# Value-weight chunks, gate scales, the phi maximum and the next attention's steps at other places in a fused attention and mixer kernel

## The chip, the cores and the metric

The kernel runs on one core of one Trainium2 chip. The metric is the device time of one execution in microseconds (us). Three runs of the kernel before gave 1181.19, 1183.59 and 1186.07 us, so the median is 1183.59 us.

## The reference, cut to what matters

There are eight batch entries of 576 rows. Each goes through three blocks, one after the other. The comments on shapes are for B = H = 8, S = 576 and D = 64.

```python
# attention through 32 memory slots per head
a = softmax(phi, axis=memory)                      # 8 8 576 32
k_m, v_m = a^T k, a^T v                            # 8 8 32 64
x = softmax(q k_m^T / 8) v_m                       # 8 8 576 64, then 8 576 512

# token mixer and a feed-forward block
u = x + (x^T U V)^T                                # U 576 32, V 32 576
x = u + relu(u w_ch1) w_ch2                        # 512 to 2048 to 512

# spatial gate
h = relu(x w_in)                                   # 512 to 1024
u, v = h[:, :512], h[:, 512:]
v_s = w_spatial layernorm(v) + b_spatial           # over the 576 rows
out = (u * v_s) w_out
```

## The kernel before, in words

All products run in float16 pairs: each operand is split into a high and a low half, and three matmuls (the list `HI`) make one product. So an eviction from PSUM is mostly two instructions, a scaled copy to the high half on ScalarE (ACT) and a scalar-tensor-tensor for the low half on VectorE (DVE).

The batch entries follow each other on TensorE (PE), in a loop over `b`. From b = 2 on all have the same stages:

- `st_phase` (L893 to L1004), twice, for the first and second half (`th`) of the 576 rows. It makes the hidden layer (the products at L933, evicted at L937 to L945 and L920/L921) and the seven products of a Strassen scheme (L899). Between these, fillers call `step(nxt)`, which issues the next piece of the next entry's attention, a generator `att` (L552 to L705). In the first half every second call of `pfill` makes a step, and in the second half `late` makes one on every second call once `y_finish` has ended.
- The value and gate halves of w_in in the order of `V_ORDER`: `v_tile` (L1083, L1086, with statistics on DVE), `v_norm` (L1139 to L1146), `u_half` (L1157, L1161), and in between the last steps of the attention.
- `spatial` (L1180 to L1207), eight pieces d of 1.7 us of matmuls each (four for each half of the rows; L1194 to L1197). A piece is finished by DVE L1202 and L1203, ACT L1204 and DVE L1205, one after the other. `g_scale` makes the gate's scale of a half: a small matmul at L159 that spreads a maximum, DVE L161, GpSimd (POOL), DVE L174 and POOL again.
- `out_half` (L1209 to L1222), four output pieces for each half.

In the last two stages stand the four value-weight chunks of the next entry: `z_chunk` (L722 to L747), 24 small matmuls at L735 into two PSUM tiles of the tag `at`, which has three buffers, evicted by two ACT instructions (L746) and two DVE instructions (L747). Each chunk then lets SP load the next piece of weights. Chunks 0, 1 and 2 are issued after pieces 0, 1 and 5 of `spatial`, chunk 3 after two of the first output pieces.

`pre(b + 2)` makes the generator of the entry after the next and runs it to its first `yield`: the maximum of phi over the rows (DVE L556, 1152 columns) and two products with the identity into a `t1k` tile (L559). The next step begins with the matmul L563, which reads this `t1k`, and DVE L565, which subtracts.

The program is recorded in this order, but a scheduler orders the instructions of each engine outside `manual_schedule` blocks. So the phi maximum, whose input is there early, was moved ahead, into the norms of the values. `tc.issue_after` holds an instruction behind another on its engine.

Of the kernel before, what the change touches and what calls it, by code (L numbers as in the profile page):

```python
# [13 lines left out]
ALU = mybir.AluOpType  # L14
AX = mybir.AxisListType
# [15 lines left out]
def mixer_kernel(  # L31
# [219 lines left out]
    AT = {}  # L251
# [300 lines left out]
    def att(b):  # L552
        a = AT[b]
        sc = a["sc"] = tp.tile([128, 24], F32, tag="sc", name="sc", bufs=2)
        mx = sc[:, 0:2]
        dve.tensor_reduce(out=mx, in_=a["phiT"], axis=AX.X, op=ALU.max)  # L556
        dgx = t1k()
        for g in range(2):
            dve.tensor_scalar(out=dgx[:, g * 128:(g + 1) * 128], in0=ident, scalar1=sc[:, g:g + 1],  # L559
                              scalar2=None, op0=ALU.mult)  # L560
        yield
        mxb = at_tile()
        pe.matmul(mxb[:, 0:256], ones32, dgx, start=True, stop=True)  # L563
# [605 lines left out]
    def g_scale(b, th):  # L1169
# [7 lines left out]
        ps2(pool, sgt, sgt, 2.0 ** 13, ALU.mult)  # L1177
        ps2(pool, isg, mg, 2.0 ** -13, ALU.mult, C("rso"), ALU.mult)

    def spatial(b, th, fill):  # L1180
        a = AT[b]
        vn = a["vn"]
        sl = slice(th * TH, (th + 1) * TH)
        if th == 0:
            a["ghl"] = tp.tile([128, 4, 2, S], F16, tag="Y", name="ghl")
        ghl = a["ghl"]
        sgt = a["ysc"][:, th * 8 + 6:th * 8 + 7]
        for d in range(4):
            ds = slice(d * 128, (d + 1) * 128)
            ps = mm_tile()[:, 0:TH]  # L1190
            i = 0
            for s in range(4):
                for x, y in HI:
                    pe.matmul(ps, vn[:, s, x, ds], wsh[:, s, th, 1 - y, :], start=(i == 0), stop=False)  # L1194
                    i += 1
            pe.matmul(ps, vn[:, 4, 0, ds], wsh[:, 4, th, 1, :], start=False, stop=False)
            pe.matmul(ps, vn[:, 4, 0, ds], wsh[:, 4, th, 0, :], start=False, stop=True)  # L1197
            if th == 0 and d in (0, 2):
                g_scale(b, d // 2)
            t = tmp()[:, 0:TH]  # L1200
            u2 = a["u2"][:, d, sl]
            dve.scalar_tensor_tensor(out=t, in0=ps, scalar=C("cvs"), in1=bb[:, sl], op0=ALU.mult, op1=ALU.add)  # L1202
            dve.tensor_tensor(out=u2, in0=t, in1=u2, op=ALU.mult)  # L1203
            act.activation(ghl[:, d, 0, sl], u2, func=ACTF.Identity, scale=sgt)  # L1204
            dve.scalar_tensor_tensor(out=ghl[:, d, 1, sl], in0=u2, scalar=sgt, in1=ghl[:, d, 0, sl],  # L1205
                                     op0=ALU.mult, op1=ALU.subtract)
            fill()  # L1207

    def out_half(b, th, ds=range(4)):  # L1209
# [225 lines left out]

    def pre(b):
        if b < B:
            gen[b] = att(b)
            next(gen[b])

# [94 lines left out]
    for b in range(B):  # L1535
        nxt = gen.get(b + 1, iter(()))
        if b == 0:
            y1, a1 = batch0()
        elif b == 1:
            sq = s_prep()  # L1540
            w1_phase(b, 0, nofill)

            def both():
                step(nxt)
                next(sq, None)

            y0 = w2_phase(b, 0, lambda: step(nxt), lambda f: fl.until(s2, min(f + 3, 16)))
            w1_phase(b, 1, nofill, y_finish(b, 0, *y0))
            y1 = w2_phase(b, 1, both)
            drain(sq)  # L1550
            load_s4()
            load_ws()
        else:
            nf = [0]

            def every(n, g):
                def f():
                    nf[0] += 1
                    if nf[0] % n == 0:
                        g()  # L1560
                return f

            y0 = st_phase(b, 0, lambda: step(nxt), every(2, lambda: step(nxt)))
            yf = y_finish(b, 0, *y0)

            def late():
                if next(yf, "end") == "end":
                    nf[0] += 1
                    if nf[0] % 2 == 0:
                        step(nxt)  # L1570

            y1 = st_phase(b, 1, nofill, late)
            drain(yf)
# [3 lines left out]
        for op in V_ORDER.split():  # L1577
            if op == "y":
                for _ in y_finish(b, 1, *y1):
                    pass  # L1580
            elif op[0] == "v":
                s = int(op[1])
                vt[s] = v_tile(b, s)
                vf()
            elif op[0] == "n":
                v_norm(b, int(op[1]), *vt[int(op[1])])
            else:
                u_half(b, int(op[1]), (int(op[2]),), vf)
        if b == 0:
            fl.finish(so)  # L1590
            vfill = lambda dt: fl(dt, a1, s1, s2)
            vf = lambda: vfill(0.1)
        else:
            drain(nxt)
            if b + 2 < B:
                load_att(b + 2)
            nz = [0]

            def vf():
                nz[0] += 1  # L1600
                if nz[0] in (1, 2, 6) and b + 1 < B:
                    z_chunk(b + 1, min(nz[0] - 1, 2), at_tile)
        spatial(b, 0, vf)
        spatial(b, 1, vf)
        if b == 0:
# [3 lines left out]
            fl.finish(so)  # L1609
            fl.finish(s1)  # L1610
        pre(b + 2)
        out_half(b, 0, range(0, 2))
        if b and b + 1 < B:
            z_chunk(b + 1, 3, at_tile)
        out_half(b, 0, range(2, 4))
        if b + 2 < B:
            step(gen[b + 2])
        for op in Z_ORDER.split():
            if op[0] == "o":
                out_half(b, 1, (int(op[1]),))  # L1620
            elif b == 0:
                z_chunk(1, int(op[1]))
        if b == 0:
            store()
        elif b + 2 < B:
            load_w1(0)
# [63 lines left out]
```

## Time and profile before

| what | us |
|---|---|
| median of three runs | 1183.59 |
| the profiled execution's own time | 1181.76 |
| its span, first to last instruction | 1180.0 |
| PE busy with matmuls | 1131.9 (96%) |
| DVE busy | 846.4 (72%) |
| ACT busy | 611.0 (52%) |
| POOL busy | 85.3 (7%) |

The profile is of one execution; times in it are microseconds from the span's start. A row of the timeline gives an instruction's start, its duration, the engine, the line, the operation and in brackets how long the engine stood idle just before and what ended that. Neighbouring instructions of one kind are merged, with their count. PEclk is the granted TensorE clock, 1.00 for 2.4 GHz and 0.50 for 1.2 GHz, as a mean over the stretch. Entry 3 (b = 3) runs from about 502 to 641 us; its norms, gate and output stages lie between 580 and 641 us.

### The profile page before, as it was taken

The numbers are of one execution on the slowest core, as the hardware profiler recorded it, in microseconds if no ns is written. First come the engines' busy times: TensorE is split into PE (matmuls) and PEld (weight loads), VectorE is DVE, ScalarE is ACT, GpSimd is POOL, SyncE is SP. The second block draws the span as 40 slices with busy tenths as digits, with TensorE's granted clock in tenths as the row PEclk, the third lists the DMA queues.
The fourth block names the chain that finished last, engine by engine and source line by source line (L and its number), as shares of the span: only waits on it lengthen the run. The fifth ranks groups of instructions, "written<-read, shape, count | busy, mean of one in ns | idle before, by whom it ended". The sixth has DMA issues, their size and how long they took to land.

```text
span 1180.0 us, 28899 instructions
## 1 busy us (share of the span) xinstructions
PE 1131.9 (96%) x12015; PEld 886.3 (75%) x12015; DVE 846.4 (72%) x2217; ACT 611.0 (52%) x1308; POOL 85.3 (7%) x316
## 2 busy tenths in 40 slices
PE   8899989999999999999989999999999999899998
PEld 6467757677668986688857987679866888579867
DVE  6767787878776777678675787757867677656854
ACT  4768754736546345454354453553544633644543
POOL 3001010000010001000010000100010000100000
PEclk9999999999999999999999999999999999999999
DMA  9879740241435230441325313252313303030211
GB/s 349 317 261 354 240 186 11 103 142 56 159 108 176 71 132 21 173 132 49 132 87 186 88 32 135 91 189 75 115 38 140 126 24 124 31 118 2 79 45 41
DMA packets 54852, 145.69 MB, mean 123 GB/s; under 512 B 7808, under 2 KB 37248, under 8 KB 43584
## 3 DMA queue, kind: packets, MB, share of 16 engines
q1 hardware_dynamic: 54208, 143.16, 34.7%
q8 instruction: 94, 1.54, 0.5%
q10 hardware_dynamic: 512, 0.67, 0.2%
q14 instruction: 38, 0.31, 0.1%
HBM read 120.32 MB, written 23.49 MB: 122 GB/s over the span
## 4 chain that ended last, share of the span: by engine, by line
PE 65%; DVE 19%; ACT 8%; DMA 3%; POOL 2%; issue 2%; ACTq 0%; POOLq 0%; DVEq 0%
PE mm L899 20%; PE mm L933 9%; PE mm L1217 7%; PE mm L1194 6%; PE mm L1086 4%; PE mm L794 3%; PE at L629 2%; PE mm L854 2%; PE at L578 2%; DVE tiny L1092 2%; PE mm L771 1%; PE mm L817 1%; PE at L735 1%; ACT gw L1139 1%; DVE yhl L1053 1%
## 5 line engine op out<-in xcount | busy, mean ns | idle before, releaser
L899 PE MATMUL mm<-gw,w2r 128*128 128x144 f16 x2304 | 169.0, 226 | 1.8 <-DVE gw L945 1.8
L899 PEld LDWEIGHTS <-w2r 128*128 128x128 f16 x2304 | 152.4, 98 | 7.4 <-issue 2.4
L933 PE MATMUL mm<-apr,z 128*128 128x288 f16 x1152 | 155.4, 286 | 2.6 <-ACT wsr L937 2.6
L933 PEld LDWEIGHTS <-z 128*128 128x128 f16 x1152 | 109.8, 98 | 31.8 <-issue 6.2
L899 PE MATMUL mm<-gw,wa 128*128 128x144 f16 x1728 | 128.8, 226 | 0.0
L937 ACT ACTIVATE wsr<-mm 128x288 f32<-128x288 f32 x192 | 78.1, 407 | 80.1 <-DVE gw L921 44.1
L899 PEld LDWEIGHTS <-wa 128*128 128x128 f16 x1728 | 111.6, 98 | 3.6 <-issue 1.0
L1194 PE MATMUL mm<-wsr,gw 128*128 128x288 f16 x768 | 110.2, 294 | 1.7 <-DVE gw L1140 1.1
L1194 PEld LDWEIGHTS <-gw 128*128 128x128 f16 x768 | 74.5, 100 | 32.3 <-issue 8.1
L1217 PE MATMUL mm<-ghl,wa 128*128 128x288 f16 x768 | 97.8, 286 | 0.0
L1157 PE MATMUL mm<-yhl,gw 128*128 128x288 f16 x768 | 97.7, 286 | 0.0
L1086 PE MATMUL mm<-gw,yhl 128*128 128x512 f16 x384 | 88.0, 385 | 5.8 <-ACT yhl L1052 5.8
L1157 PEld LDWEIGHTS <-gw 128*128 128x128 f16 x768 | 74.1, 98 | 24.1 <-issue 6.1
L1217 PEld LDWEIGHTS <-wa 128*128 128x128 f16 x768 | 74.4, 98 | 22.8 <-issue 3.8
L1204 ACT ACTIVATE ghl<-gw,ysc 128x288 f16<-128x288 f32 x64 | 34.2, 535 | 104.8 <-DVE gw L1203 83.1
L939 DVE TENSOR_TENSOR wsr<-wsr 128x288 f32<-128x288 f32 x96 | 44.0, 458 | 58.5 <-ACT wsr L937 58.5
L921 DVE TENSOR_TENSOR gw<-wsr,gw 128x720 f16<-128x720 f32 x96 | 85.5, 901 | 0.0
L920 ACT ACTIVATE gw<-wsr 128x720 f16<-128x720 f32 x96 | 76.4, 796 | 3.9 <-DVE wsr L941 3.4
L1086 PEld LDWEIGHTS <-yhl 128*128 128x128 f16 x384 | 36.7, 99 | 50.8 <-ACT yhl L1052 6.6
L794 PE MATMUL mm<-gw,w2r 128*128 128x288 f32 x256 | 65.9, 409 | 0.0
L794 PEld LDWEIGHTS mm<-gw,w2r 128*128 128x128 f32 x256 | 47.5, 190 | 15.1 <-issue 1.5
L1092 DVE BATCH_NORM_STATS2 tiny<-tmp 128x6 f32<-128x512 f32 (+1 forms) x40 | 25.6, 639 | 43.0 <-ACT tmp L1090 43.0
(311 smaller groups left out, 1916.6 us busy)
## 6 DMA issues: line engine op xcount, KB each, us to landing
wa<-w1d SPq DMA_DIRECT2D x22, 1024.0 KB, 4.9
kvt<-in_kv_dram SPq DMA_DIRECT2D x28, 516.0 KB, 5.3
gw<-wid SPq DMA_DIRECT2D x12, 1024.0 KB, 8.1
wsr<-wsd SPq DMA_DIRECT2D x7, 1440.0 KB, 7.8
out_dram<-tmp SPq DMA_DIRECT2D x64, 144.0 KB, 1.9
qt<-in_qT_dram SPq DMA_DIRECT2D x28, 256.0 KB, 3.6
gw<-in_w_dram SPq DMA_DIRECT2D x6, 1024.0 KB, 9.3
wa<-wod SPq DMA_DIRECT2D x6, 1024.0 KB, 4.7
```

The lines of the kernel that those rows point to most:

```text
L794: pe.matmul(ps, w2r[:, f, d * 128:(d + 1) * 128], AT[0]["g"][:, f, :], start=False, stop=(f == 15))
L899: pe.matmul(ps[:, dd * QH:(dd + 1) * QH], w(c, dd, 1 - x), gs[:, m, c, y, :], start=(first and c == 0 and dd == 0 and i == 0), stop=(end a ...
L920: act.activation(h, X[:, 3:8], func=ACTF.Copy)
L921: dve.tensor_tensor(out=gs[:, 2:7, c, 1, :], in0=X[:, 3:8], in1=h, op=ALU.subtract)
L933: pe.matmul(ps, a["z"][:, k, x, f * 128:(f + 1) * 128], a["apr"][:, k, y, sl], start=(i == 0), stop=(i == 5))
L937: act.activation(o, pair(ps), func=ACTF.Relu, scale=CG)
L939: dve.tensor_tensor(out=X[:, 4:6], in0=X[:, 2:4], in1=X[:, 1:3], op=ALU.subtract)
L1086: pe.matmul(ps, yhl[:, k, x, s * 128:(s + 1) * 128], wih[:, k, 0, 1 - y, :], start=(i == 0), stop=(i == 11))
L1092: dve.bn_stats(bs, v)
L1157: pe.matmul(ps, wih[:, k, 1, 1 - x, d * 128:(d + 1) * 128], a["yhl"][:, k, y, sl], start=(i == 0), stop=(i == 11))
L1194: pe.matmul(ps, vn[:, s, x, ds], wsh[:, s, th, 1 - y, :], start=(i == 0), stop=False)
L1217: pe.matmul(ps, (wo0 if b else woh)[:, k, 1 - x, d * 128:(d + 1) * 128], a["ghl"][:, k, y, sl], start=(i == 0), stop=(i == 11))
```

## The change

Six edits, all of place and order; the number of instructions on PE, DVE, ACT and POOL stays the same.

1. Value chunk 0 of the next entry is issued ahead of `spatial`, chunks 1 and 2 after pieces 2 and 6, chunk 3 after three output pieces.
2. `g_scale` of the first half moves into the u pieces (after u12), that of the second half from piece 2 to piece 1 of `spatial`.
3. The phi maximum and its two products are held behind the last DVE instruction of the last `spatial` piece.
4. The first half of `st_phase` makes no attention steps from call 19 on; the count then starts anew, and `late` makes a step on two calls of three.
5. The step with L563 comes after out piece 3 of the first half as before, but for entry 0 after everything else.
6. The last 64 rows of q get their own place in `gw`, for b above 2, and are loaded when `pre` runs.

```diff
@@ att @@
-        dve.tensor_reduce(out=mx, in_=a["phiT"], axis=AX.X, op=ALU.max)
         dgx = t1k()
-        for g in range(2):
-            dve.tensor_scalar(out=dgx[:, g * 128:(g + 1) * 128], in0=ident, scalar1=sc[:, g:g + 1],
-                              scalar2=None, op0=ALU.mult)
+        with ExitStack() as es:
+            if behind_ghl:
+                es.enter_context(tc.issue_after(behind_ghl[0]))
+            dve.tensor_reduce(out=mx, in_=a["phiT"], axis=AX.X, op=ALU.max)
+            for g in range(2):
+                dve.tensor_scalar(out=dgx[:, g * 128:(g + 1) * 128], in0=ident, scalar1=sc[:, g:g + 1],
+                                  scalar2=None, op0=ALU.mult)
@@ spatial @@
-            if th == 0 and d in (0, 2):
-                g_scale(b, d // 2)
+            if th == 0 and d == 1:
+                g_scale(b, 1)
...
-            dve.scalar_tensor_tensor(out=ghl[:, d, 1, sl], in0=u2, scalar=sgt, in1=ghl[:, d, 0, sl],
-                                     op0=ALU.mult, op1=ALU.subtract)
+            behind_ghl[:] = [dve.scalar_tensor_tensor(out=ghl[:, d, 1, sl], in0=u2, scalar=sgt, in1=ghl[:, d, 0, sl],
+                                                op0=ALU.mult, op1=ALU.subtract).ins]
@@ pre @@
         if b < B:
+            if b > 2:
+                t = AT[b]["q"][4] = gw[:, 8064:8320].rearrange("p (g c) -> p g c", g=4)
+                sp.dma_start(t, qT[b, :, :, 512:S])
@@ the loop over b @@
-            y0 = st_phase(b, 0, lambda: step(nxt), every(2, lambda: step(nxt)))
+            y0 = st_phase(b, 0, lambda: step(nxt), every(2, lambda: nf[0] < 19 and step(nxt)))
+            nf[0] = 0
...
-                    if nf[0] % 2 == 0:
+                    if nf[0] % 3:
                         step(nxt)
...
                 u_half(b, int(op[1]), (int(op[2]),), vf)
+                if op == "u12":
+                    g_scale(b, 0)
...
+            if b + 1 < B:
+                z_chunk(b + 1, 0, at_tile)
             nz = [0]
             def vf():
                 nz[0] += 1
-                if nz[0] in (1, 2, 6) and b + 1 < B:
-                    z_chunk(b + 1, min(nz[0] - 1, 2), at_tile)
+                if nz[0] in (3, 7) and b + 1 < B:
+                    z_chunk(b + 1, nz[0] // 3, at_tile)
...
-        out_half(b, 0, range(0, 2))
+        out_half(b, 0, range(0, 3))
         if b and b + 1 < B:
             z_chunk(b + 1, 3, at_tile)
-        out_half(b, 0, range(2, 4))
-        if b + 2 < B:
+        out_half(b, 0, range(3, 4))
+        if 0 < b and b + 2 < B:
             step(gen[b + 2])
...
         if b == 0:
+            if B > 2:
+                step(gen[2])
```

The orders that the scheduler makes of this are shown for DVE, the engine that PE waits for, in entry 3. The lines of the changed kernel stand 3 higher from L563 to L1180 and 4 to 5 higher elsewhere (L556 is now L560, L559 is L562, L747 is L750, L1202 is L1207, L1205 is L1210).

The first place is the norms of values 2 and 3. L556 and L559 are the phi maximum and its products, L1092 and L1098 the statistics of a value tile, L151 and L153 the operand `dgb` of a small matmul L159 that closes the attention of the next entry. Before:

```order
L1092 BN_STATS tiny<-tmp 128x6
L556 TENSOR_REDUCE sc<-phiT 128x2
L1098 BN_AGGR mv<-tiny 128x2
L559 TENSOR_SCALAR t1k<-ident,sc 128x128 x2
L151 TENSOR_SCALAR tiny<-tiny 128x1
L153 TENSOR_SCALAR dgb<-identb,tiny 128x128
L1092 BN_STATS tiny<-tmp 128x6
L1098 BN_AGGR mv<-tiny 128x2
```

and with the change:

```order
L1095 BN_STATS tiny<-tmp 128x6
L165 TENSOR_REDUCE tiny<-at 128x1
L1101 BN_AGGR mv<-tiny 128x2
L692 TENSOR_REDUCE tiny<-tiny 128x1
L1095 BN_STATS tiny<-tmp 128x6
L1101 BN_AGGR mv<-tiny 128x2
L151 TENSOR_SCALAR tiny<-tiny 128x1
L153 TENSOR_SCALAR dgb<-identb,tiny 128x128
```

The phi maximum has left this place. The last window maximum of the attention (L165) and its sum-up (L692) came in, and `dgb` now stands behind the statistics of value 3.

The second place is the start of `spatial`, from the gate scale to piece 2. L747 is the low half of a value chunk. Before:

```order
L1166 TENSOR_REDUCE tiny<-tiny 128x1
L151 TENSOR_SCALAR tiny<-tiny 128x1
L153 TENSOR_SCALAR dgb<-identb,tiny 128x128
L1202 SCALAR_TENSOR_TENSOR tmp<-mm,st,bb 128x288
L161 TENSOR_REDUCE tiny<-mm 128x1
L1203 TENSOR_TENSOR gw<-tmp,gw 128x288
L174 RECIPROCAL ysc<-ysc 128x1
L1205 SCALAR_TENSOR_TENSOR ghl<-gw,ysc,ghl 128x288
L747 SCALAR_TENSOR_TENSOR z<-at,z 128x512 x2
```

and with the change:

```order
L723 SCALAR_TENSOR_TENSOR vmu<-t1k,rq,vmu 128x256
L161 TENSOR_REDUCE tiny<-mm 128x1
L174 RECIPROCAL ysc<-ysc 128x1
L1169 TENSOR_REDUCE tiny<-tiny 128x1
L151 TENSOR_SCALAR tiny<-tiny 128x1
L153 TENSOR_SCALAR dgb<-identb,tiny 128x128
L750 SCALAR_TENSOR_TENSOR z<-at,z 128x512 x2
L1207 SCALAR_TENSOR_TENSOR tmp<-mm,st,bb 128x288
L1208 TENSOR_TENSOR gw<-tmp,gw 128x288
L1210 SCALAR_TENSOR_TENSOR ghl<-gw,ysc,ghl 128x288
```

The first half's gate scale (L161, L174) and chunk 0 now stand ahead of piece 0; before, piece 0 had the scale between its instructions and chunk 0 behind it.

The third place is the end of `spatial`, from piece 6 on. Before:

```order
L747 SCALAR_TENSOR_TENSOR z<-at,z 128x512 x2
L1202 SCALAR_TENSOR_TENSOR tmp<-mm,st,bb 128x288
L1203 TENSOR_TENSOR gw<-tmp,gw 128x288
L1205 SCALAR_TENSOR_TENSOR ghl<-gw,ysc,ghl 128x288
L1202 SCALAR_TENSOR_TENSOR tmp<-mm,st,bb 128x288
L1203 TENSOR_TENSOR gw<-tmp,gw 128x288
L1205 SCALAR_TENSOR_TENSOR ghl<-gw,ysc,ghl 128x288
L747 SCALAR_TENSOR_TENSOR z<-at,z 128x512 x2
L565 TENSOR_TENSOR e<-e,at 128x1024
```

and with the change:

```order
L750 SCALAR_TENSOR_TENSOR z<-at,z 128x512 x2
L1207 SCALAR_TENSOR_TENSOR tmp<-mm,st,bb 128x288
L1208 TENSOR_TENSOR gw<-tmp,gw 128x288
L1210 SCALAR_TENSOR_TENSOR ghl<-gw,ysc,ghl 128x288
L560 TENSOR_REDUCE sc<-phiT 128x2
L562 TENSOR_SCALAR t1k<-ident,sc 128x128 x2
L750 SCALAR_TENSOR_TENSOR z<-at,z 128x512 x2
L568 TENSOR_TENSOR e<-e,at 128x1024
```

The phi maximum now stands behind the last gate piece and ahead of chunk 3. On PE the matmul that reads its `t1k` (L563 before, L566 now) keeps its place: behind the fourth output piece and ahead of the second half's four, as instruction row 6609 of PE's order in entry 2 in both kernels.

## Rows read from the trace of the kernel before

**Rows 1.** Waits of PE: engine, line, whom it waited for: us, times, longest.

```profile
PE at L735 <- DVE z L747: 13.1, 6, 2.2
PE mm L159 <- DVE dgb L153: 6.1, 6, 1.2
...
PE mm L933 <- ACT wsr L937: 2.6, 10, 0.3
...
PE mm L899 <- DVE gw L945: 1.8, 5, 0.4
```

**Rows 2.** Timeline of PE in entry 3, norms to output.

```profile
597.82 0.22 PE L159 MATMUL mm<-dgb,onesb 128*128 128x128 bf16 x1 [1.17 <-DVE dgb L153]
...
611.84 0.39 PE L735 MATMUL at<-wa,vmt 64*32 64x512 f16 x1
614.42 1.27 PE L735 MATMUL at<-wa,vmt 64*32 64x512 f16 x23 [2.19 <-DVE z L747]
615.63 2.83 PE L1194 MATMUL mm<-wsr,gw 128*128 128x288 f16 x12
...
628.05 3.10 PE L1217 MATMUL mm<-ghl,wa 128*128 128x288 f16 x24
...
634.81 0.59 PE L563 MATMUL at<-t1k,ones 128*128 128x256 f32 x2
```

**Rows 3.** Windows of 24 us round the chunks of entries 1 to 6; columns in the first row.

```profile
core 0: us, PE busy (x) PEld busy (x) DVE busy (x) ACT busy (x) POOL busy (x), PEclk, DMA share, GB/s
327.00:351.00 24.00, 21.47 (x223) 14.98 (x221) 18.39 (x52) 12.59 (x30) 3.31 (x13) 1.00 0.35 123
466.00:490.00 24.00, 21.48 (x224) 14.97 (x222) 19.14 (x51) 11.32 (x27) 2.40 (x9) 1.00 0.36 132
604.00:628.00 24.00, 21.47 (x210) 14.27 (x208) 18.78 (x50) 11.35 (x27) 2.43 (x9) 0.93 0.36 118
743.00:767.00 24.00, 21.47 (x210) 14.45 (x208) 18.47 (x49) 11.71 (x27) 2.64 (x11) 0.93 0.31 111
882.00:906.00 24.00, 21.47 (x209) 14.44 (x208) 18.38 (x51) 12.12 (x28) 2.93 (x12) 0.93 0.29 102
1022.00:1046.00 24.00, 20.50 (x212) 13.83 (x210) 18.74 (x51) 11.87 (x28) 2.79 (x11) 1.00 0.39 132
```

**Rows 4.** Timeline of DVE in entry 3, norms to output.

```profile
595.27 1.33 DVE L556 TENSOR_REDUCE sc<-phiT 128x2 f32<-128x1152 f32 x1
...
596.64 0.83 DVE L559 TENSOR_SCALAR t1k<-ident,sc 128x128 f32<-128x128 f32 x2
...
597.51 0.25 DVE L153 TENSOR_SCALAR dgb<-identb,tiny 128x128 bf16<-128x128 bf16 x1
...
610.50 0.51 DVE L1202 SCALAR_TENSOR_TENSOR tmp<-mm,st,bb 128x288 f32<-128x288 f32 x1
...
613.68 1.29 DVE L747 SCALAR_TENSOR_TENSOR z<-at,z 128x512 f16<-128x512 f32 x2
...
620.87 0.51 DVE L1202 SCALAR_TENSOR_TENSOR tmp<-mm,st,bb 128x288 f32<-128x288 f32 x1
...
622.47 0.52 DVE L1205 SCALAR_TENSOR_TENSOR ghl<-gw,ysc,ghl 128x288 f16<-128x288 f32 x1 [0.60 <-ACT ghl L1204]
622.91 0.51 DVE L1202 SCALAR_TENSOR_TENSOR tmp<-mm,st,bb 128x288 f32<-128x288 f32 x1
...
626.55 1.29 DVE L747 SCALAR_TENSOR_TENSOR z<-at,z 128x512 f16<-128x512 f32 x2
```

**Rows 5.** Page, part 6: loads of value weights; count, KB, us to landing.

```profile
wa<-w1d SPq DMA_DIRECT2D x22, 1024.0 KB, 4.9
```

**Rows 6.** Timeline of DVE in entry 3, from one half to the other.

```profile
540.57 0.69 DVE L633 TENSOR_REDUCE tinyw<-at 128x16 f32<-128x512 f32 x1 [0.51 <-PE at L629]
...
546.28 0.69 DVE L651 TENSOR_TENSOR ahl<-tmp,ahl 128x512 f16<-128x512 f32 x1
```

**Rows 7.** Window in the second half of entry 3; columns as in rows 3.

```profile
571.00:580.00 9.00, 9.00 (x155) 8.67 (x153) 5.99 (x16) 1.22 (x3) 0.00 (x0) 1.00 0.68 258
```

More of the change, by code (lines that the diff above doesn't have):

```diff
@@ L1178, in g_scale @@
         ps2(pool, isg, mg, 2.0 ** -13, ALU.mult, C("rso"), ALU.mult)
+    behind_ghl = []
     def spatial(b, th, fill):
```

## The prediction

> **What bounds the kernel now.** I read the waits of PE first. PE works nearly all the time: in the stretches that matter it is busy 21.47 of 24 us [rows 3]. So only its own idle time and its own clock can be won, and the reader should ask of each wait which engine ends it. The list is short [rows 1]: 13.1 us at the value chunks (six waits of up to 2.2 us), 6.1 us at the small matmul L159, and 2.6 and 1.8 us in the hidden layer. All but the third are ended by DVE, and that one by ACT, which waits there for DVE.
>
> The timeline of PE in entry 3 shows the first two [rows 2]. Chunk 1 of the values gets one matmul done at 611.84 and then stands until 614.42, 2.58 us from start to start, since its second PSUM tile is one that chunk 0 used and DVE has not emptied it. DVE gets there only at 613.68, behind the first gate piece [rows 4]. L159 waits 1.17 us for `dgb`, which DVE writes at 597.51, behind 1.33 and 0.83 us of the phi maximum [rows 4], work that nobody needs for another 37 us.
>
> The windows round the chunks show a third loss [rows 3]: the clock is 1.00 in entries 1, 2 and 6 and 0.93 in 3, 4 and 5. In 24 us that is 1.7 us lost at half clock. In entry 3 the twelve matmuls right behind the wait take 2.83 us [rows 2]. So a wait of 2.2 us drew a stretch at 1.2 GHz behind it in three of six cases.
>
> **The change part by part, entry 3 as the pattern.**
>
> *Chunk 0 ahead of the pieces, chunk 1 behind piece 2.* Chunk 1 now comes three pieces, over 5 us, after chunk 0, and DVE empties chunk 0 ahead of piece 0. The wait of 2.58 us goes, and with it the slow stretch. The weights of a chunk are loaded once the chunk before is through, 4.9 us to landing [rows 5]; chunks 1 and 2 will be four pieces apart, chunks 2 and 3 a piece and three output pieces, about 6 us. I cost that at nothing; the cover is about 1 us, and if a landing is later than that, PE waits for the rest.
>
> *Phi maximum held back.* DVE reaches `dgb` without the 2.16 us. But `dgb` now stands behind the statistics of value 3, so I leave 0.2 of the 1.17 us, and take 1.0. In entry 6 there is no phi maximum left to move.
>
> *What is late next.* The phi maximum doesn't vanish. Its result is read by L563, which keeps its place on PE, ahead of the second half's four output pieces, and everything behind it on PE waits. So the question is when DVE has done the gate, three chunks and the phi maximum, and when PE gets to L563.
>
> PE: today the output pieces start at 628.05 and L563 at 634.81 [rows 2], 6.76 us for four pieces and a chunk. Without 1.0, 2.58 and 1.7 us, and with 0.2 us less at the last norms, the output starts at 622.6 and L563 is reached at 629.3.
>
> DVE: a gate piece by itself takes 2.04 us from one L1202 to the next (620.87 to 622.91), 0.60 of it idle for ACT's L1204; two that overlap take 3.64 (622.91 to 626.55); the evictions of a chunk take 1.29, or about 1.25 with the next one behind [rows 4]. In the new order pieces 0, 3, 4 and 7 stand alone, 1 with 2 and 5 with 6 overlap. So: three chunks 3.75, four pieces 8.16, two pairs 7.28, the second gate scale 0.5 (an estimate: its trip through POOL is mostly covered by the pair), and the phi maximum 2.16. That is 21.85 us from DVE's start on chunk 0.
>
> Where does it start? The trace has the first gate piece on DVE at 610.50 [rows 4]. It could be 2.16 us earlier, 608.3, if all of the phi work came off; it could be as late as 613.7, where chunk 0 is emptied today. I take 610.2: some 1.2 us come off, since part of the phi work ran while DVE would have waited for ACT, and 0.9 us are added by the gate scale's trip through POOL, now ahead of the chunk. So L563 starts at 610.2 + 21.85 = 632.05, and PE stands there for about 2.75 us. Against 634.81 that is 2.75 us earlier, of which 1.7 are the clock and 1.05 the rest. Of the 3.8 us of waits removed in this stage, most come back as one wait at L563.
>
> After that wait the clock can fall again. The rows know only the six waits of 2.2 us, with three slow stretches; I take half of five, at 1.7 us. [...] Half of five costs 4.3 us, all five 8.5.
>
> *Attention steps thinned out.* In the first half one group of the softmax goes: seven DVE instructions from 540.57 to 546.28, some 3.9 us with their own lengths [rows 6], right where the hidden layer of the second half starts and waits. The waits at L933 and L899, 2.6 and 1.8 us over entries 2 to 6 [rows 1], should go: 4.4 us. The group lands in the second half, where DVE is busy 5.99 of 9 us while PE has no gap [rows 7]. So 3.0 us are free for 3.9 us of work, with the last matmuls that read it moved a little later as well; I cost this at nothing, and its upper bound is a rival. The own tile of the last q rows only lets them be loaded early: on SP the load stands behind the last reading of the values by `spatial`, ahead of the output stores, the first of which is due 1.5 us later, so nothing waits behind it.
>
> *Gate scale earlier.* It takes POOL's trip out of piece 0. That is inside the DVE sum above.
>
> **The sum.** L563 earlier by 1.05 us in entries 1 to 5: 5.25. Slow stretches removed in entries 3 to 5: 5.1. Entry 6, which has no phi and so no new wait, keeps the whole chunk wait: 2.6. Hidden layer: 4.4. New slow stretches: minus 4.3. Together 13.05 us. The profiled execution took 1181.76 us and would take 1168.7; the median of the runs lies 1.83 us above it, at 1183.59, so I forecast 1170.5 us.
>
> **The rivals.** Half a per cent, 5.9 us, is about what a measurement of this kernel can tell from no change: faster means below 1177.7, slower above 1189.5.
>
> - *DVE keeps up.* If the pieces overlap more than in the trace, L563 finds its data. For it speaks that 0.60 us of each single piece is idle [rows 4]; against it, that the order fixes which pieces overlap. Five waits of 2.75 and the 4.3 fall away: 1152.5 us.
> - *Every new wait is followed by half clock.* Then the sum loses 4.25 more: 1174.7 us. For it: the new waits are longer than those that did so in three of six cases. Against: three cases of six did not. [...]
> - *The softmax group in the second half is not hidden.* It is the input of ten small matmuls (L660) close to the end of that half, and the scale of y stands behind it on DVE. Of 3.9 us, 3.0 are free [rows 7], and two trips to ACT are added. If PE is held for 1.5 us in each of five entries, 7.5 us: 1178.0 us.
> - *Slower: DVE starts late on the gate.* If the scale's trip through POOL, the last norms and ACT's share of chunk 0 put DVE on chunk 0 only at 613.7, where it stands today, the phi result comes at 635.5. L563 is then 0.7 us later than now in entries 3 to 5 and 2.4 us later in 1 and 2, 6.9 us together, and waits of 6 us would all be followed by half clock, 8.5 us. With 4.4 and 2.6 won, that is 8.4 us lost: 1192.0 us. Each microsecond of delay costs 5 us, so it decides from about 612 to 613 on. For it: DVE is the engine that everything here waits for. Against: the phi work is gone from in front.
>
> **How the numbers follow.** The forecast gets 0.52, DVE keeping up 0.12, all at half clock 0.14, the softmax 0.12, the late start 0.08, and 0.02 is left for what I don't see. Faster: 0.52, 0.12, 0.14 and a quarter of the softmax case, 0.81. Slower: most of the late start, 0.07. The rest, 0.12, is within half a per cent. The range runs from the case where DVE keeps up, 1153, to beyond the softmax case, 1182, since the start of DVE's chain may lie a microsecond off either way, 5 us in the sum. It leaves out the late start and part of the first rival.
>
> **What would show it.** Right: in the waits of PE, L735 and L159 nearly gone, and a new one at the phi matmul, ended by DVE's `t1k`, five times some 2.75 us; the waits in the hidden layer of the second half gone; the half clock no longer behind a chunk, but in some entries behind the phi matmul; DVE's pieces still 2.0 us alone and 3.6 us in pairs. Wrong: no wait at the phi matmul (DVE faster than I took it), a wait at L660 or at the scale of y (the softmax), a wait of a chunk for its weights, or L159 still waiting over 0.5 us.

## The result, and the profile after

The changed kernel takes 1164.24 us (median of four runs, 1161.08 to 1165.22) against 1183.40 us before (a fourth run lowered its median by 0.2): a ratio of 0.983, 95% interval 0.980 to 0.986. That is 19 us less; the forecast was 1170.5 us in a range of 1153 to 1182. The profiled execution took 1165.14 us with a span of 1163.4, against 1180.0 before: 16.6 us less.

The waits of PE after the change:

```profile
PE at L566 <- DVE t1k L562: 11.4, 5, 2.4
...
PE mm L1199 <- ACT gw L1164: 1.6, 3, 1.1
...
PE mm L159 <- DVE dgb L153: 0.8, 2, 0.6
```

The four waits of [rows 1] are gone or nearly so: none at the chunks (13.1 us before), none in the hidden layer (2.6 and 1.8), 0.8 left of 6.1 at L159. In their place stands one new wait, in five entries, at the matmul that reads the phi maximum. Entry 3 shows it on PE:

```profile
622.96 1.04 PE L738 MATMUL at<-wa,vmt 64*32 64x512 f16 x24
623.93 1.65 PE L1222 MATMUL mm<-ghl,wa 128*128 128x288 f16 x12
628.02 0.83 PE L566 MATMUL at<-t1k,ones 128*128 128x256 f32 x2 [2.44 <-DVE t1k L562]
628.64 1.65 PE L1222 MATMUL mm<-ghl,wa 128*128 128x288 f16 x6
```

Twelve matmuls take 1.65 us ahead of the wait, and behind it six do: the clock has fallen to 1.2 GHz. The windows of 12 us round the wait, entries 1 to 5 (columns as in [rows 3]):

```profile
351.00:363.00 12.00, 10.38 (x101) 7.53 (x99) 6.19 (x11) 6.38 (x14) 0.55 (x1) 1.00 0.54 175
488.00:500.00 12.00, 9.56 (x63) 6.85 (x61) 5.00 (x8) 6.02 (x14) 0.55 (x1) 0.86 0.53 174
624.00:636.00 12.00, 9.55 (x62) 6.78 (x63) 5.59 (x10) 5.94 (x12) 0.55 (x1) 0.86 0.51 163
762.00:774.00 12.00, 9.56 (x64) 6.91 (x62) 5.00 (x8) 6.09 (x14) 0.55 (x1) 0.86 0.54 175
899.00:911.00 12.00, 9.56 (x99) 7.23 (x97) 5.46 (x9) 7.26 (x16) 0.55 (x1) 1.00 0.64 193
```

A mean of 0.86 over 12 us is 1.7 us lost, in entries 2, 3 and 4. Round the chunks, where PE was busy 21.47 of 24 us at 0.93 in entry 3 [rows 3], it is now busy 23.89 at 1.00:

```profile
600.00:624.00 24.00, 23.89 (x262) 16.64 (x261) 19.40 (x47) 11.11 (x26) 2.12 (x8) 1.00 0.39 138
```

And DVE in entry 3, from chunk 0 to the phi result that L566 waits for:

```profile
606.20 1.28 DVE L750 SCALAR_TENSOR_TENSOR z<-at,z 128x512 f16<-128x512 f32 x2
...
613.49 1.29 DVE L750 SCALAR_TENSOR_TENSOR z<-at,z 128x512 f16<-128x512 f32 x2
614.70 0.51 DVE L1207 SCALAR_TENSOR_TENSOR tmp<-mm,st,bb 128x288 f32<-128x288 f32 x1
...
616.74 0.51 DVE L1207 SCALAR_TENSOR_TENSOR tmp<-mm,st,bb 128x288 f32<-128x288 f32 x1
...
622.42 1.29 DVE L750 SCALAR_TENSOR_TENSOR z<-at,z 128x512 f16<-128x512 f32 x2
...
625.66 1.35 DVE L560 TENSOR_REDUCE sc<-phiT 128x2 f32<-128x1152 f32 x1
627.04 0.83 DVE L562 TENSOR_SCALAR t1k<-ident,sc 128x128 f32<-128x128 f32 x2
```

The two groups of [rows 4], which ran at 595.27 in the norms, now end this chain, 21.7 us after its start at 606.20.

The hidden layer of entry 3, as the first matmuls of it and of the values behind it; before, and then after:

```profile
501.46 1.63 PE L933 MATMUL mm<-apr,z 128*128 128x288 f16 x12
...
579.99 1.89 PE L1086 MATMUL mm<-gw,yhl 128*128 128x512 f16 x8
```

```profile
499.04 1.14 PE L936 MATMUL mm<-apr,z 128*128 128x288 f16 x8
...
575.99 1.89 PE L1089 MATMUL mm<-gw,yhl 128*128 128x512 f16 x8
```

It went from 78.53 to 76.95 us with the same matmuls; over entries 2 to 6 from 391.8 to 384.7. So 7.0 of the 16.6 us come from the hidden layer. Measured from the first value matmul of an entry to the next entry's hidden layer, entries 1 to 5 give 4.7 us together (the clock included): 0.3, -0.6, 1.0, 1.1 and 2.8. Entry 6 gives 3.9, and entry 7 takes back 0.3. The last 1.4 us lie ahead of entry 1's values, which begin at 301.97 instead of 303.37. There two waits are gone in which PE stood for DVE at entry 0's chunks, 1.17 and 0.23 us. The longer one, before:

```profile
215.08 0.37 PE L735 MATMUL mm<-wa,vmt 64*32 64x512 f16 x1 [1.17 <-DVE z L747]
```

Edit 5 moved the step with L563 out of their way: in entry 0 it stood at 210.32 ahead of these chunks and now comes at 219.93 behind them. It was not tried alone, but the run further down with the first edit alone keeps these waits (1.4 us), and the runs that undo edits 1, 2, 3 or 4 have none of over 0.2 us there.

### The profile page after: what moved, and what is told of

It is laid out like the page before. It is cut to its first block, busy times and chain, and to the rows that moved or that the text cites. A ratio compares the mean times of both kernels' runs of the same rounds, so it can differ in the third digit from the quotient of the medians.

```text
span 1163.4 us, 28931 instructions
## 1 busy us (share of the span) xinstructions
PE 1128.4 (97%) x12012; PEld 884.8 (76%) x12015; DVE 845.4 (73%) x2217; ACT 609.2 (52%) x1308; POOL 85.5 (7%) x316
## 4 chain that ended last, share of the span: by engine, by line
PE 65%; DVE 20%; ACT 7%; DMA 2%; POOL 2%; issue 2%; SPq 0%; ACTq 0%; POOLq 0%; DVEq 0%
PE mm L902 22%; PE mm L936 12%; PE mm L1222 6%; PE mm L797 4%; PE mm L1089 4%; PE mm L1199 3%; PE at L632 2%; ACT ghl L1209 2%; PE mm L857 2%; DVE tiny L1095 2%; DVE z L750 2%; DVE ghl L1210 2%; PE at L581 2%; DVE gw L1208 1%; DVE gw L1143 1%
## 5 line engine op out<-in xcount | busy, mean ns | idle before, releaser
L902 PE MATMUL mm<-gw,w2r 128*128 128x144 f16 x2304 | 168.8, 226 | 0.0
L902 PEld LDWEIGHTS <-w2r 128*128 128x128 f16 x2304 | 152.4, 98 | 5.0
L936 PE MATMUL mm<-apr,z 128*128 128x288 f16 x1152 | 155.0, 286 | 0.0
L936 PEld LDWEIGHTS <-z 128*128 128x128 f16 x1152 | 109.7, 98 | 28.2 <-issue 2.0
L902 PE MATMUL mm<-gw,wa 128*128 128x144 f16 x1728 | 127.9, 226 | 0.0
L902 PEld LDWEIGHTS <-wa 128*128 128x128 f16 x1728 | 111.2, 98 | 3.5 <-issue 1.0
L1199 PE MATMUL mm<-wsr,gw 128*128 128x288 f16 x768 | 104.7, 286 | 1.6 <-ACT gw L1164 1.6
L1222 PE MATMUL mm<-ghl,wa 128*128 128x288 f16 x768 | 102.1, 294 | 0.0
L1199 PEld LDWEIGHTS <-gw 128*128 128x128 f16 x768 | 73.4, 98 | 27.3 <-issue 9.6
```

The source lines that it names most:

```text
L902: pe.matmul(ps[:, dd * QH:(dd + 1) * QH], w(c, dd, 1 - x), gs[:, m, c, y, :], start=(first and c == 0 and dd == 0 and i == 0), stop=(end a ...
L936: pe.matmul(ps, a["z"][:, k, x, f * 128:(f + 1) * 128], a["apr"][:, k, y, sl], start=(i == 0), stop=(i == 5))
L1222: pe.matmul(ps, (wo0 if b else woh)[:, k, 1 - x, d * 128:(d + 1) * 128], a["ghl"][:, k, y, sl], start=(i == 0), stop=(i == 11))
```

## The experiments

The theory at this point: what the chunks and the norms gave up comes back as a wait at L566, since DVE's chain bounds this stage. Four runs undo or move one thing each.

**The thinned steps undone.**

```diff
-            y0 = st_phase(b, 0, lambda: step(nxt), every(2, lambda: nf[0] < 19 and step(nxt)))
-            nf[0] = 0
+            y0 = st_phase(b, 0, lambda: step(nxt), every(2, lambda: step(nxt)))
...
-                    if nf[0] % 3:
+                    if nf[0] % 2 == 0:
```

> The changed kernel with its thinned steps undone: the softmax group runs in the first half of the hidden layer again, all else as changed. Theory: the hidden-layer stages of entries 2 to 6, which became 7.0 us shorter, owe this to the steps alone. Then the waits at L936 and L902 are back (about 4.4 us over five entries), the stage is 6.4 to 7 us longer in all, and the time is about 1171 us (against 1164.2). Rival: part of the 7.0 us comes from the own q tile (loads that are issued earlier), which stays here. Then only the 4.4 us of waits come back: about 1168.6 us. A third way: DVE has less to do in the second half and reaches the end of the stage earlier; the time is then below 1168.

Measured: 1168.79 us (1167.70 to 1169.64), ratio to before 0.987 [0.985, 0.989], 4.5 us slower than the change. PE's waits:

```profile
PE at L566 <- DVE t1k L562: 7.6, 5, 1.6
PE mm L1199 <- ACT gw L1164: 7.1, 8, 1.1
...
PE mm L159 <- DVE dgb L153: 3.8, 7, 0.6
PE mm L936 <- ACT wsr L940: 2.6, 10, 0.3
...
PE mm L902 <- DVE gw L948: 1.8, 5, 0.4
```

The hidden-layer waits are back to the tenth, and the stage with them (78.22 us in each of entries 2 to 6). So 6.4 of the 7.0 us are the steps'; the other 0.6, in entries 3 and 6, stay without them. But the time moved by 4.5 only: the wait at L566 gave 3.8 us back and no half clock follows it, while 8.5 us more of waits stand at L159 and L1199, in front of L566, so that PE comes there later. The time is the rival's number, 1168.6, but not by the rival's reason: the stage lost the theory's 6.4 us, and something was given back elsewhere.

**The phi maximum not held back.**

```diff
-            if behind_ghl:
-                es.enter_context(tc.issue_after(behind_ghl[0]))
```

> The changed kernel without the hold-back of the phi maximum, so that it runs on DVE between the last norms again, in front of the input of the small matmul L159. Theory (DVE bounds the stage, and a piece of its work only changes the place where PE waits for it): the wait at L566 (11.4 us in five entries, and three half-clock stretches of 1.7 us) goes; the wait at L159 comes back with about 1.2 to 2 us in each of five entries, and DVE starts on the gate about 1 us later, which the chunks' new places should cover. Sum: minus 16.5, plus 6 to 10, so 6 to 10 us faster than the change, about 1154 to 1158 us; at least no slower. Rival (the hold-back itself won time): slower than the change by the 5 to 6 us that L159 cost before, about 1170 us.

Measured: 1154.74 us (1152.88 to 1157.18), ratio 0.975 [0.973, 0.977], 9.5 us faster than the change. The wait at L566 is gone, and L159 waits again:

```profile
PE mm L159 <- DVE dgb L153: 11.6, 11, 1.9
```

The time is within the theory's range. So 11.4 us of waits at one place became 10.8 more at the other; the gain is the half clock, 5.1 us, which follows none of these, and the 1.6 us at L1199, which went too. The remaining 2 us would be the time that PE takes to fill again behind a wait; that part is argued. By itself the hold-back doesn't pay: it moved a wait of 1.9 us to a place where it came out at 2.44 us and cost clock as well.

**The chunks at their old places.**

```diff
-            if b + 1 < B:
-                z_chunk(b + 1, 0, at_tile)
...
-                if nz[0] in (3, 7) and b + 1 < B:
-                    z_chunk(b + 1, nz[0] // 3, at_tile)
+                if nz[0] in (1, 2, 6) and b + 1 < B:
+                    z_chunk(b + 1, min(nz[0] - 1, 2), at_tile)
...
-        out_half(b, 0, range(0, 3))
+        out_half(b, 0, range(0, 2))
```

> The changed kernel with the four value chunks at their old places (behind gate pieces 0, 1 and 5, the last behind two output pieces). Theory (DVE bounds the stage): the chunk's wait of about 2 us is back in entries 1 to 6, but the wait at L566 shrinks by as much in entries 1 to 5, since DVE's work up to the phi maximum is the same. What is lost is entry 6 (2.6 to 3.9 us) and what the clock makes of it: about 1167 to 1169 us. Rival (the chunks' move is worth the wait that it removes): 13 us of waits and three half-clock stretches of 1.7 us come back beside the wait at L566: about 1180 us.

Measured: 1168.14 us (1164.33 to 1170.08), ratio 0.985 [0.983, 0.988], 3.9 us slower than the change and within the theory's range. The two waits changed places:

```profile
PE at L738 <- DVE z L750: 10.1, 6, 2.2
...
PE at L566 <- DVE t1k L562: 1.0, 3, 0.3
```

With the rest of the change in place, PE pays for DVE's lateness once, either at a chunk or at L566. The clock, too, was lost three times again (0.93 over windows of 26 us in entries 3, 5 and 6), now behind the chunk.

**The phi matmul behind the second output piece of the second half.**

```diff
-        if 0 < b and b + 2 < B:
-            step(gen[b + 2])
...
+                if op == "o1" and 0 < b and b + 2 < B:
+                    step(gen[b + 2])
```

> The changed kernel with the step that holds the phi matmul (L566) moved behind the second of the second half's four output pieces on PE; DVE's order stays. Theory A (the wait at L566 is one of place only: DVE's result comes 2.4 us late, and the output pieces that PE could do meanwhile need only the ghl that DVE has finished before the phi maximum): the five waits of 11.4 us, their refill and three half-clock stretches of 1.7 us go, about 16 us: 1148 us. Theory B (DVE bounds the stage whatever PE does): PE meets DVE again at the second half's output pieces, whose last ghl was written 2.8 us before the phi result, or at the next matmuls that read the phi scale; the gain is half or less: 1156 to 1164 us.

Measured: 1148.02 us (1145.66 to 1150.19), ratio 0.969 [0.967, 0.972], 16.2 us faster than the change: theory A to the microsecond. PE in entry 3:

```profile
619.32 1.04 PE L738 MATMUL at<-wa,vmt 64*32 64x512 f16 x24
620.29 4.58 PE L1222 MATMUL mm<-ghl,wa 128*128 128x288 f16 x36
624.71 0.59 PE L566 MATMUL at<-t1k,ones 128*128 128x256 f32 x2
625.14 3.10 PE L1222 MATMUL mm<-ghl,wa 128*128 128x288 f16 x24
```

No wait, no gap, and no output piece behind it waits for DVE. In each entry the phi result is now there at least 0.48 us before PE comes to L566. So "DVE bounds the stage" was too strong: DVE was late for one small result, and PE had other work to do.

The next runs ask how far the chain of DVE alone sets the wait, and what the edits do singly.

**The gate scales at their old places.**

```diff
-            if th == 0 and d == 1:
-                g_scale(b, 1)
+            if th == 0 and d in (0, 2):
+                g_scale(b, d // 2)
...
-                if op == "u12":
-                    g_scale(b, 0)
```

> The changed kernel with the two gate scales at their old places (behind gate pieces 0 and 2). Theory (DVE's chain from chunk 0 to the phi result sets L566): the first scale's trip through POOL stands inside the chain again instead of ahead of it, so the wait at L566, 2.44 us an entry, grows by 0.5 to 1 us in each of five entries: 2 to 5 us slower than the change, 1166 to 1169 us. Rival: the scale is out of the way at either place (DVE does another piece meanwhile): no difference, 1164 us.

Measured: 1153.42 us (1153.23 to 1154.92), ratio 0.975 [0.972, 0.978], 10.8 us faster than the change. Theory and rival both fall. The wait, and DVE in entry 3:

```profile
PE at L566 <- DVE t1k L562: 8.2, 5, 1.7
```

```profile
601.92 1.28 DVE L750 SCALAR_TENSOR_TENSOR z<-at,z 128x512 f16<-128x512 f32 x2
...
609.48 1.29 DVE L750 SCALAR_TENSOR_TENSOR z<-at,z 128x512 f16<-128x512 f32 x2
610.69 0.51 DVE L1207 SCALAR_TENSOR_TENSOR tmp<-mm,st,bb 128x288 f32<-128x288 f32 x1
...
617.30 1.29 DVE L750 SCALAR_TENSOR_TENSOR z<-at,z 128x512 f16<-128x512 f32 x2
...
621.93 0.83 DVE L562 TENSOR_SCALAR t1k<-ident,sc 128x128 f32<-128x128 f32 x2
```

Here pieces 3 to 6 take 6.61 us (610.69 to 617.30) and overlap all four; in the changed kernel they take 7.72 (614.70 to 622.42), with pieces 3 and 4 alone, 2.0 us each. The chain from chunk 0 to the end of L562 is 20.84 us against 21.67. The wait falls from 2.44 to 1.7 us, and at 1.7 no half clock follows in any entry. Of the 10.8 us, 3.2 are the waits at L566 (11.4 less 8.2) and 5.1 the clock; 2.2 are waits of the changed kernel at L1199 and L159 that went too, so the early scale also cost PE time ahead of the chain. Why the scheduler overlaps fewer pieces with the scales in front can't be read from a trace; that it does is what the rows show.

**The phi maximum written twice, at both places of the matmul.** The maximum is made twice with the same result; first in the changed kernel, then in the one with the later matmul.

```diff
             dve.tensor_reduce(out=mx, in_=a["phiT"], axis=AX.X, op=ALU.max)
+            dve.tensor_reduce(out=mx, in_=a["phiT"], axis=AX.X, op=ALU.max)
```

> The changed kernel with the phi maximum written twice: one more DVE instruction of 1.35 us in front of the result that L566 waits for. Theory (nothing but DVE's chain ends that wait): each of five waits grows from 2.4 to 3.8 us, 6.8 us in all, and with the two waits that so far drew no half clock up to 3.4 us more: 1171 to 1174.5 us. Rival (the wait is ended by something else, or DVE has idle time that takes the instruction): at most 2 us slower.

Measured: 1177.56 us (eight runs, 1173.24 to 1179.05), ratio 0.994 [0.992, 0.996], 13.3 us slower than the change. The waits grew by 6.9 us, as forecast (the line is now L567), the one in entry 1 from 1.62 to 3.01 and the other four from 2.44 to 3.83. The clock cost more:

```profile
PE at L567 <- DVE t1k L563: 18.3, 5, 3.8
```

```profile
350.00:364.00 14.00, 10.99 (x92) 7.49 (x90) 11.05 (x19) 6.31 (x13) 0.55 (x1) 0.88 0.57 198
492.00:506.00 14.00, 10.17 (x98) 7.30 (x96) 8.28 (x13) 6.52 (x14) 0.55 (x1) 1.00 0.46 150
630.00:644.00 14.00, 10.17 (x73) 7.22 (x67) 7.06 (x11) 5.99 (x13) 0.55 (x1) 0.88 0.44 145
768.00:782.00 14.00, 10.17 (x75) 6.60 (x60) 7.52 (x12) 5.44 (x11) 0.55 (x1) 0.76 0.39 128
908.00:922.00 14.00, 10.17 (x81) 7.26 (x67) 7.28 (x12) 6.04 (x13) 0.55 (x1) 0.88 0.43 146
```

Four of five entries lose clock, the fourth twice as much (0.24 of 14 us is 3.4 us lost). In these entries the clock loses 3.4 us more than in the changed kernel; with the longer waits that is 10.3 us, the upper end of the theory's range. The other 3 us stand in front: the chunks of entry 1 begin at 332.9 us here and at 329.6 in the changed kernel. Most of them were lost in the start-up of this execution: entry 0's first value matmul comes at 161.78 us and not at 159.41. There PE waits 1.07 us for a load of q at 18.46 us, and less clock is granted. The first 45 us, in the changed kernel and here:

```profile
0.00:45.00 45.00, 37.18 (x327) 25.93 (x328) 30.85 (x70) 23.71 (x45) 12.11 (x32) 0.96 0.83 310
0.00:45.00 45.00, 39.10 (x320) 29.36 (x321) 28.73 (x67) 21.38 (x43) 12.16 (x32) 0.89 0.78 294
```

A mean of 0.89 instead of 0.96 over 45 us is 3.2 us of lost clock, part of which other waits take up. The second maximum runs for the first time at 91.91 us, so this loss is not its work.

> The kernel with the phi matmul behind the second output piece, with the phi maximum written twice as well. There the phi result is ready 0.49 us before PE comes to L566. Theory (the move bought that cover and no more): 1.35 less 0.49 is a wait of about 0.86 us in each of five entries, 4.3 us and some refill, and no half clock, since waits of up to 1.6 us at this place drew none: 1152 to 1154 us. Rival A (DVE bounds the stage, so that every added us is paid): 6.8 us, 1155 us or more. Rival B (DVE has more room than the order shows): 1148 us.

Measured: 1152.74 us (1151.44 to 1154.46), ratio 0.974 [0.970, 0.977], 4.7 us slower than without the second maximum: the theory. The cover of 0.49 us is used up, and the rest is a wait of 0.9 us without half clock, in four entries and not in five: entry 1 had 1.3 us of cover.

```profile
PE at L567 <- DVE t1k L563: 3.6, 4, 0.9
```

**The first edit alone, on the kernel before.** The diff is the reverse of the third experiment's, on the kernel before.

> The kernel before with the first edit alone: chunk 0 ahead of the gate pieces, chunks 1 and 2 behind pieces 2 and 6, the last behind the third output piece. The phi maximum stays between the norms, the steps, the scales and the q tile as before. Theory: the six chunk waits (13.1 us), their refill and three half-clock stretches of 1.7 us go, and no wait takes their place, since the phi result is there long before L563: 1163 to 1166 us, as fast as the whole change, whose other parts then cancel out. Rival (DVE bounds the stage, and reaches chunk 0 and the pieces late because the phi maximum stands before them): a wait of 1 to 2 us comes back at a chunk or an output piece: 1170 to 1176 us.

Measured: 1158.64 us (1155.16 to 1159.38), ratio 0.978 [0.975, 0.982]: 24.5 us faster than before, and faster than the whole change. It is 4 us under the theory's range, which had counted the chunk waits, their refill and the clock. Of these 4 us, 2.2 are waits for the norms that went too, at L1194 and L1196, 2.4 us before and 0.2 here. The waits of [rows 1] stand there unchanged, but for the chunks; the one left at L735 is that of entry 0:

```profile
PE mm L159 <- DVE dgb L153: 6.1, 6, 1.2
...
PE mm L933 <- ACT wsr L937: 2.6, 10, 0.3
...
PE mm L735 <- DVE z L747: 1.4, 2, 1.2
```

```profile
592.00:616.00 24.00, 24.00 (x250) 17.64 (x249) 19.95 (x68) 12.65 (x31) 3.77 (x15) 1.00 0.31 104
```

The rival falls: DVE keeps up with the gate although the phi maximum stands before it.

**Two together, and two crossed.** The next two kernels put the gate scales at their old places: one in the kernel with the later phi matmul, the other in the kernel without the hold-back.

> Two experiments together: the phi matmul behind the second output piece, and the gate scales at their old places. Theory: each of the two alone ended what the wait at L566 cost (the one by place, the other by a DVE chain that is 1.2 us shorter and by a wait too short to draw half clock), so together they don't add up; what is left are the small waits at L159 and the 1.6 us wait, and no half clock: 1145 to 1148 us, at most 3 us better than the later matmul alone (1148.0). Rival (the gains add: 16 and 11 us): about 1138 us.

Measured: 1144.97 us (1143.30 to 1145.16), ratio to before 0.967 [0.964, 0.969], the fastest kernel of this study, 19 us below the changed one. As expected the gains don't add: 3 us on top of the later matmul, the lower edge of the theory's range.

> The kernel with the phi maximum between the norms, and the gate scales at their old places as well: of the change only the chunks' places, the thinned steps and the q tile are left. Theory (the scales matter only through the length of DVE's chain in front of L566, which here has no wait): the wait at L159 stays 1.2 to 1.9 us an entry, and the time is that of the kernel without the hold-back, 1154.7, or the kernel with chunks alone (1158.6) less the 6.4 us of the hidden layer: 1151 to 1155 us. Rival (the scale's early place costs time by itself, as it delays DVE ahead of chunk 0): 5 us or more below 1154.7.

Measured: 1150.65 us (1150.32 to 1152.65), ratio 0.972 [0.969, 0.974], just under the theory's range. The scale's early place costs by itself: L159 waits 7 times and 9.5 us here, and 11 times and 11.6 us with the early scale. The four runs give a table of the two edits on top of the chunks, steps and q tile:

| | scales at the old places | scales earlier |
|---|---|---|
| phi maximum in the norms | 1150.65 | 1154.74 |
| phi maximum held back | 1153.42 | 1164.24 |

Each edit alone costs 3 to 4 us, both together 13.6. Of the 6.7 us more than the sum, 5.1 are three half-clock stretches, which of these four kernels only the one with the waits of 2.44 us has.

**The steps undone in the fastest kernel.** The diff is that of the first experiment.

> The fastest kernel so far (later phi matmul, gate scales at their old places, 1145.0) with the thinned steps undone. There no wait at L566 is left that could give something back. Theory (the steps are worth what the hidden layer shows, 78.22 less 76.95 us in each of five entries, less what their side effect in the value stage adds, 28.36 against 26.66 us with the steps undone in the changed kernel): 6.4 to 14.9 us slower, 1151 to 1160 us; the lower end if the waits at L159 and L1199 in the value stage came from the scale's early place, the upper end if the steps alone bring them. Rival (the steps are worth no more than the 4.4 us of waits listed before): 1149.4 us.

Measured: 1156.03 us (1154.12 to 1157.52), ratio 0.978 [0.975, 0.980], 11.1 us slower by the medians and 8.9 by the profiled spans (1152.3 against 1143.4). The hidden layer's two waits are back as in the first experiment, 2.6 us at L936 and 1.8 at L902. At L1199 there is none and at L159 one of 0.2 us. So in the first experiment those came from the early scale together with the old steps; the later phi matmul, the other difference, had changed neither (1.6 and 0.8 us with it and without).

Its hidden layer takes 392.1 us over entries 2 to 6, against 384.8 in the fastest kernel: 7.3 of the 8.9 us, 0.6 of it a wait of entry 3 for a load of q. The time is within the theory's range and off the rival's. The median's difference is 2 us larger than the spans'. The profiled execution is the fastest of the four and had the highest mean clock, 0.998 against 0.996 to 0.997, a difference of 1 to 2 us over this span; whether that is all of it stays open.

## Why the prediction was right, and where it wasn't

**The place of the new wait: right.** The waits went where the prediction said, at all four old places, and one came, in the five entries named, for `t1k`. The chain on DVE was worked out as 21.85 us and measured as 21.7; the wait as 2.75 and measured as 2.44 in entries 2 to 5. Put on the clock of [rows 2] (this entry runs 4.0 us earlier), the output pieces began at 622.46 (618.46 in its own trace) and L566 at 632.02; 622.6 and 632.05 were forecast. Pieces alone (2.04) and in pairs kept the durations taken. Without the clock, entries 2 to 5 gave 1.0 to 1.1 us each, where 1.05 was taken. The runs with the phi maximum twice show that nothing else ends that wait. The chunks' weights [rows 5], costed at nothing, made PE wait nowhere in these entries.

**Entry 1 and entry 0: not seen, and they cancel by luck.** In entry 1 the stage gave 0.3 us and not 1.05. New waits stand there that the prediction had not listed, 1.12 us at L1199, where PE waits for ACT, and 0.6 at L159, which is one of the signs of being wrong that it had named. With the scales at their old places no wait is left at L1199 and 0.2 us at L159, so they come with the early gate scale. Entries 1 to 5 were to give 5.25 + 5.1 - 4.3 = 6.05 us and gave 4.7, mainly for 0.7 less in entry 1 and 0.8 less for the clock. Edit 5 was given no term at all; it goes with the 1.4 us won in entry 0, which happen to make up for what is missing.

**The clock: the term was near, and the rival at full half clock did not come.** Half of five stretches was taken, three were measured in the profiled execution. The rival in which every new wait is followed by half clock does not hold here: the waits of 2.44 us drew it in three of four entries, the first one, of 1.62 us, did not, nor did any of up to 1.7 us in the runs with the steps undone or the scales at their old places. The waits of 3.0 to 3.8 us drew it four times in five. The Trainium skill ("TensorE: Matmul & The Clock Gate", "What's actually happening") says that the throttled state is the default and that activity releases it. The traces agree in the direction, as each fall in these entries comes with or just behind a wait of PE; which wait draws it they don't settle.

**The hidden layer: mis-sized.** "The waits at L933 and L899 should go: 4.4 us" took the listed waits alone. The stage gave 7.0: 6.4 from the steps, since a wait also costs the matmuls their overlap behind it (one at L902 in the last experiment is 0.35 us of idle time and 0.58 us from start to start, where these matmuls otherwise follow each other in 0.06), and 0.6 that stayed with the steps undone in the first experiment. Those lie in the two entries whose weight loads for L629 waited for q, 0.2 and 0.3 us, and may be the own q tile's; it was not tried alone, and one such wait, 0.6 us, was back in the last experiment with the tile in place. The softmax group in the second half cost nothing, as taken; that rival falls.

**Entry 6: mis-sized**, 2.6 taken and 3.9 measured. The chunk's wait was the largest part, but two more waits for the norms left with it, which the prediction had not listed. The waits of PE before, from 998 to 1057 us:

```profile
PE at L735 <- DVE z L747: 2.1, 1, 2.1
PE mm L1194 <- DVE gw L1140: 1.1, 2, 0.5
PE mm L1196 <- DVE gw L1146: 0.2, 1, 0.2
```

The sum of 13.05 and the 16.6 us of the spans differ by 3.6: 2.6 more in the hidden layer, 1.3 more in entry 6 and 1.4 from entry 0, less the 1.4 missing in entries 1 to 5 and the 0.3 that entry 7 took back. The other 2.7 of the 6.3 us between forecast and result lie between executions: 1.8 us that I added from the profiled execution to the median before, and 0.9 by which the profiled execution after lies above its own median.

**What each part is worth: not seen.** The sum gave the chunks and the hold-back their gains together and set one new wait against them. The runs separate them: chunks alone bring 24.5 us on the kernel before (within the change, with the waits trading places, 3.9), and the hold-back costs 2.8 or 9.5 us as long as L566 keeps its place. With L566 moved it pays: 1144.97 us with it against 1150.65 without (there L566 keeps its place, where it has nothing to wait for). "*Gate scale earlier.* It takes POOL's trip out of piece 0. That is inside the DVE sum above" is the step that failed as a judgement of an edit: the sum had the right chain for the whole, but I never worked out the chain without that edit, which is 0.8 us shorter by the rows. The time of the rival in which DVE keeps up, 1152.5 us, is near what the change takes with either of these two edits left out, 1153.4 and 1154.7 us, but not by that rival's mechanism: PE still waits for DVE there, 8.2 us at L566 in the one and 11.6 us at L159 in the other, and what fell away is mostly the half clock.

The late start of DVE, the slower rival, did not come: chunk 0 started at 606.20, which is 610.2 on the clock of [rows 4], since this entry runs 4.0 us earlier by its first value matmul (575.99 against 579.99). It is the value taken.

## What to carry to other kernels

When an edit moves work behind a deadline to clear a wait in front, ask first who reads the result, and whether that reader can be moved as well: moving one step on PE was worth 16 us here, and DVE's order stayed as it was. Price each edit of a bundle alone against the same chain, also those that look free; two that cost 3 and 4 us cost 13.6 together, mostly since only the longest waits of the four kernels drew half clock as well. Read a wait in the list neither as what it costs nor as what its removal brings: 4.4 us listed in the hidden layer cost 6.4, and 13.1 us listed at the chunks brought 24.5 us alone and 3.9 within the change, where another wait stood ready to take their place.

## What the runs showed of the hardware that was not expected

Longer waits of PE for DVE drew the half clock more often, but no length that was seen always did: of the five waits of 1.5 to 1.7 us with the scales at their old places, none; of the 2.2 us waits in the kernel before, three of six; of the four of 2.44 us, three; of the five of 3.0 to 3.8 us, four. Waits of 1.9 us went either way: two of four drew it at the chunks with their old places, none of four at L159 without the hold-back. One stretch cost 1.7 us, before and after; only behind one of the 3.8 us waits it was twice that.

The clock also differs between executions. The runs of the changed kernel had mean granted clocks of 0.993 to 0.997, and the one at 0.997 is the fastest, 1161.08 us. Over the first 45 us, which no edit between them touches, it was 0.96 in the profiled execution of the changed kernel, 0.89 with the phi matmul moved and 1.00 with the steps undone, and entry 0's first value matmul came at 159.41, 161.24 and 158.69 us. So a difference of 2 us between two single executions can be start-up alone.

The same two L566 matmuls took 0.59 us without a wait in front, 0.67 behind a wait at full clock (entry 5) and 1.19 where the clock had fallen (entry 4); the 0.83 us of entry 3 are partly at either level.
